# Routing lists with 64-byte records instead of 8-byte ones, filled by one DMA, in an attention-then-mixture-of-experts kernel

## The chip, the cores and the metric

The kernel runs on one core of a Trainium2 chip. The metric is the device time of one launch in microseconds, lower is better. The engines meant below are TensorE (PE in the profile), VectorE (DVE), ScalarE (ACT), GpSimd (POOL) and SyncE (SP). SP issues most of the plain DMAs; GpSimd issues the indirect ones, whose row addresses come from a tile of indices.

## The reference

Linear attention with decay, in float32, for 4 batches, 8 heads, 768 positions and head size 64, followed by a noisy top-2 mixture of experts on the 3072 resulting rows of 512 (8 experts, hidden size 1024):

```python
x = attn_out.transpose(0, 2, 1, 3).reshape(B * S, H * D)      # 3072 x 512
logits = x @ w_gate
noise_scale = np.log1p(np.exp(x @ w_noise))
noisy_logits = logits + noise_scale * noise
top2 = np.argpartition(-noisy_logits, 2, axis=1)[:, :2]
# top2_w: softmax over the two chosen logits
for e in range(E):
    for k in range(2):
        mask = top2[:, k] == e
        h = np.maximum(x[mask] @ w1[e], 0.0)
        out[mask] += top2_w[mask, k, None] * (h @ w2[e])
```

## The kernel before, in words

**Attention** runs in 12 steps of 256 rows (the loop `for t in range(NST)`, a unit u is a step's two chunks of 128 rows). A step transposes k and q of the next unit on TensorE (L298, L311), computes the decayed state (L386, L395, L398) and the scores (L339), multiplies the scores by a decay mask on VectorE (L342), forms the output (L351), transposes it back (L414) and stores the rows to the DRAM tensor `x_tok` (L418). GpSimd scales k for the state (`kdecay`, L327). In each step SP loads k, q and v of the unit three steps ahead.

**Routing** is done in three batches of 8 chunks (`GB`). `gate` (VectorE) computes the noisy logits and the two best experts per row; `weights` (GpSimd, with one reciprocal on VectorE at L507) computes the two softmax weights; `count` and `route` (TensorE and VectorE) give each pair of row and expert a place in that expert's list. Then `scatter_list` (L556) writes the records: one indirect DMA on GpSimd per chunk and choice, so 16 per batch and 48 in all, each with 128 records. A record is the row's number and its weight, `RW` = 2 words of 4 bytes. The lists lie in one DRAM tensor `lst` of 8 lists of 3712 records; before the first scatter they are filled with an out-of-range row number and weight 0 (L876, in step 4, on SP's queue, from the tile `linit`).

**Experts.** Tiles of 128 records are worked on per expert: `load_rec` (L723, L725) loads records from the list, `gather_rows` (L729) fetches the 128 rows of `x_tok` that they name, `trans_rows` (L738, L740, L741) transposes them and splits them into a high and a low part, `gemm1` (L754, L760, L764) and `gemm2` (L792) multiply, and `scatter_out` (L811) adds the result into the output. Expert 0 is worked on in three parts of 2, 2 and 3 tiles (`PARTS0`), each fed by the routing batch of the same number: part 0 is gathered on GpSimd right after the first batch's scatters, at attention step 10 (`GX`); part 1 after the second batch's, part 2 and the other experts after the third. The records reach GpSimd as the indices of a gather only after the list load has landed, and the list load waits for the scatters to land.

**Order.** The schedule is written out by hand: every engine runs its instructions in the order in which the program issues them, and waits come from data only. Several routing instructions are interleaved into the attention steps by `advance(n)`.

**Warm-up.** `keep_warm` (L174) issues matmuls on a tile of zeros, `idle`, 14 of them at the start, so that TensorE is busy while the first loads arrive. `warm` is a one-column tile on which ScalarE does its first activation (L166). A separate tile `zero` of 512 columns, set by GpSimd (L821), is the source of the output's zero fill (L827) and of ScalarE's clearing of gather tiles (L913).

Lines such as L556 are lines of the kernel before; the changed kernel numbers its own up to four lower.

Of the kernel before, what the change touches and what calls it, by code (L numbers as in the profile page):

```python
# [21 lines left out]
FT = mybir.dt.float32  # L22
FR = mybir.dt.float32r
BF = mybir.dt.bfloat16
I32 = mybir.dt.int32
U32 = mybir.dt.uint32
AF = mybir.ActivationFunctionType
OP = mybir.AluOpType
# [7 lines left out]
DM = H * D  # L36
DB = DM // 128
E = 8
# [12 lines left out]
CAP = FULL + TAIL  # L51
STRIDE = 3712
OV = 128
RW = 2
SPS = 6
NST = NCH // 2
NW = NC // 2
# [10 lines left out]
GB = (0, 8, 16, NCH)  # L68
NG = len(GB) - 1
GM = max(GB[i + 1] - GB[i] for i in range(NG))  # L70
# [17 lines left out]
def sub(ap, offset, dims):  # L88
    return bass.AP(tensor=ap.tensor, offset=ap.offset + offset, ap=dims)
# [31 lines left out]
def kernel(  # L121
# [3 lines left out]
    nc = tc.nc  # L125
# [13 lines left out]
    lst = dram.tile([E * STRIDE, RW], I32, name="lst")  # L139
# [21 lines left out]
        nc.sync.dma_start(store[u].rearrange("p h x d -> p h (x d)"),  # L161
                          sub(src, at, [[2 * D, 128], [S * D, H], [1, 2 * D]]))

    warm = ac.tile([128, 1], FT, name="warm")
    nc.vector.memset(warm, 0.0)
    nc.scalar.activation(warm, warm, AF.Copy)  # L166
    idle = ac.tile([128, 384], BF, name="idle")
    nc.vector.memset(idle, 0.0)

    def keep_warm(n):  # L170

# [48 lines left out]
    for nm in ("kt", "qt", "vt"):  # L220
# [7 lines left out]
    ones = consts.tile([128, 128], BF, name="ones")  # L228
    nc.gpsimd.memset(ones, 1.0)
    ST = [ac.tile([128, HP, D], FT, name=f"S{i}") for i in range(5)]  # L230
    iota8 = consts.tile([128, 2, GM, E], FT, name="iota8")
    nc.gpsimd.iota(iota8, pattern=[[0, 2], [0, GM], [1, E]], base=0, channel_multiplier=0,
                   allow_small_or_imprecise_dtypes=True)
    tokf = consts.tile([128, NCH], FT, name="tokf")
    nc.gpsimd.iota(tokf, pattern=[[C, NCH]], base=0, channel_multiplier=1,
                   allow_small_or_imprecise_dtypes=True)
    LI = E * STRIDE // 128 // 4
    linit = ac.tile([128, LI, RW], I32, name="linit")
    nc.gpsimd.memset(linit, BIG)
    nc.gpsimd.memset(linit[:, :, 1:2], 0)  # L240
    sel = consts.tile([128, 2 * E], FT, name="sel")
# [191 lines left out]
    def gate(b):  # L433
        v = nc.vector
        gs = GB[b + 1] - GB[b]
        sh = [128, gs, E]
        t = lambda sh, nm, dt=FT: rp.tile(sh, dt, name=nm)
        pl = PL[b]
        l2 = t([128, gs, 16], "l2")
        v.tensor_copy(l2, pl[:, :gs, :])  # L440
        yield
        zc = t(sh, "zc")
        v.tensor_scalar(zc, l2[:, :, 8:16], 87.0, -87.0, op0=OP.min, op1=OP.max)
        yield
        z = zc.rearrange("p c e -> p (c e)")
        fl = [128, gs * E]
        a = t(fl, "ga")
        v.scalar_tensor_tensor(a, z, -1.0, z, op0=MULT, op1=OP.max)
        yield
        e = t(fl, "ge")  # L450
        yield from exp_neg(v, rp, e, a, fl, "g")
        acc = t(fl, "glacc")
        v.tensor_scalar(acc, e, LOGC[-1], None, op0=MULT)
        yield
        for c in LOGC[-2::-1]:
            v.scalar_tensor_tensor(acc, acc, c, e, op0=ADD, op1=MULT)
            yield
        acc3 = acc.rearrange("p (c e) -> p c e", e=E)
        v.scalar_tensor_tensor(acc3, l2[:, :, 8:16], 0.0, acc3, op0=OP.max, op1=ADD)
        yield  # L460
        nl = t(sh, "nl")
        v.tensor_mul(nl, acc.rearrange("p (c e) -> p c e", e=E), nz[:, GB[b]:GB[b + 1], :])
        yield
        v.tensor_add(nl, nl, l2[:, :, 0:8])
        yield
        mx = t(sh, "mx")
        mi = t(sh, "mi", U32)
        for c in range(gs):
            v.max(mx[:, c, :], nl[:, c, :])
            yield  # L470
        for c in range(gs):
            v.max_index(mi[:, c, :], mx[:, c, :], nl[:, c, :])
            yield
        ei = t([128, 2, gs], "ei")
        v.tensor_copy(ei.rearrange("p r c -> p c r"), mi[:, :, 0:2])
        yield
        oh = t([128, 2, gs, E], "oh")
        v.tensor_tensor(oh, iota8[:, :, :gs, :], ei[:, :, :, None].to_broadcast([128, 2, gs, E]), op=OP.is_equal)
        yield
        ob = t(sh, "ob", BF)  # L480
        v.tensor_add(ob, oh[:, 0], oh[:, 1])
        yield
        RT[b] = dict(mx=mx, ei=ei, oh=oh, ob=ob)

    def weights(b):
        v = nc.gpsimd
        gs = GB[b + 1] - GB[b]
        sh = [128, gs, E]
        r = RT[b]
        t = lambda sh, nm, dt=FT: rp.tile(sh, dt, name=nm)  # L490
        mx = r["mx"]
        rec = r["rec"] = rp.tile([128, gs, 2, RW], I32, name="rec", bufs=2)
        for i in range(2):
            v.tensor_copy(rec[:, :, i, 0], tokf[:, GB[b]:GB[b + 1]])
            yield
        a = t([128, gs], "wa")
        v.tensor_tensor(a, mx[:, :, 0], mx[:, :, 1], op=SUB)
        yield
        v.tensor_scalar(a, a, 87.0, None, op0=OP.min)
        yield  # L500
        e = t([128, gs], "we")
        yield from exp_neg(v, rp, e, a, [128, gs], "w", fused=False)
        s = t([128, gs], "ws")
        v.tensor_scalar(s, e, 1.0, 1e-9, op0=ADD, op1=ADD)
        yield
        yield "sum"
        nc.vector.reciprocal(s, s)  # L507
        yield
        recf = rec.bitcast(FT)
        v.tensor_copy(recf[:, :, 0, 1], s)  # L510
        v.tensor_mul(recf[:, :, 1, 1], e, s)
# [305 lines left out]
            tc.declare_no_dep(st.ins, s.ins, reason="an expert has a token once")  # L817
        out_st.append(st)

    zero = consts.tile([128, DM], FT, name="zero")  # L820
    nc.gpsimd.memset(zero, 0.0)  # L821

    zeros = iter(range(NTOK // 128))

    def zero_out(n):
# [3 lines left out]
    for t in range(NST):  # L829
        u = t + 1  # L830
        if u < NST:
            trans_k(u)
        load(t + 3, "kt")
        if u < NST:
            trans_q(u)
        load(t + 3, "qt")
        if u < NST:
            kv(u)
            state(u)
            advance(FILLS)  # L840
        else:
            store_x(t - 1)
            products(t - 1)
            logits(t - 1)
        intra(t)
        load(t + 3, "vt")
        inter(t, 0)
        evac_o(t)
        if u < NST:
            if t:  # L850
                store_x(t - 1)
                products(t - 1)
            scores(u)
            inter(u, 1)
            if t:
                logits(t - 1)
        if 2 * t in GB[1:]:
            jobs.append(routing(GB.index(2 * t) - 1))
        kdecay(t + 2)
        scatter(SPS)  # L860
        if t in SPLITS:
            split_w(SPLITS[t][0], 0, SPLITS[t][1])
        advance(FILL - (SPLIT if t in SPLITS else 0))
        if t == GX:
            scatter(sum(job[0] == 0 for job in scatters))
            assert "done" in RT[0]
            load_rec(0, 0, nc.gpsimd)
            for j in range(PARTS0[0]):
                gather_rows(0, j, GB[1] * C)
        if t in LOADS:  # L870
            load_w(LOADS[t][0], 0, LOADS[t][1])
        if t == 2:
            nc.sync.dma_start(nz, sub(noise, 0, [[E, 128], [128 * E, NCH], [1, E]]))
        if t == 4:
            for i in range(4):
                nc.sync.dma_start(sub(lst, i * 128 * LI * RW, [[LI * RW, 128], [1, LI * RW]]), linit)  # L876
    products(NST - 1)
    for j in range(2):
        trans_rows(j, TS)
# [232 lines left out]
```

## Time and profile before

| | |
|---|---|
| median of 3 runs | 810.88 us (806.73, 810.88, 1853.96) |
| span of the profiled execution | 803.7 us |
| its own time | not listed apart; the nearest run shown is 806.73 us, 3.0 us above the span |
| PE, DVE, ACT, POOL busy | 743.7, 325.1, 222.4, 290.9 us |
| mean granted TensorE clock | 0.958 |
| DMA moved | 103.49 MB, 92667 packets |
| DMA queue "instruction" (q8) | 49 packets, 0.80 MB |

The span runs from the first to the last instruction. A busy TensorE is not one at its peak, since matmuls are pipelined. Times on the timeline are microseconds from the span's start: attention runs to about 170 us, expert 0 from there to some 275 us with the routing of the second and third batch beside it, the other seven experts to the end. The granted clock is TensorE's share of full speed. "issue" as the releaser of an idle time means that the profile shows nothing that the engine waited for.

### The profile page before, as it was taken

The numbers are of one execution on the slowest core, as the hardware profiler recorded it, in microseconds if no ns is written. First come the engines' busy times: TensorE is split into PE (matmuls) and PEld (weight loads), VectorE is DVE, ScalarE is ACT, GpSimd is POOL, SyncE is SP. The second block draws the span as 40 slices with busy tenths as digits, with TensorE's granted clock in tenths as the row PEclk, the third lists the DMA queues.
The fourth block names the chain that finished last, engine by engine and source line by source line (L and its number), as shares of the span: only waits on it lengthen the run. The fifth ranks groups of instructions, "written<-read, shape, count | busy, mean of one in ns | idle before, by whom it ended". The sixth has DMA issues, their size and how long they took to land. (4 is left out here: it accounts for less than half of the span.)

```text
span 803.7 us, 15438 instructions
## 1 busy us (share of the span) xinstructions
PE 743.7 (93%) x6122; PEld 626.0 (78%) x6122; DVE 325.1 (40%) x742; ACT 222.4 (28%) x381; POOL 290.9 (36%) x474
## 2 busy tenths in 40 slices
PE   6999898685959999999999999999999999999993
PEld 4888776474758889889888888888788888889882
DVE  5555654353412554436243424433342443335210
ACT  0445443241111343214222321322142232214100
POOL 1321155547755145442344234333413433221221
PEclk8899998697979999999999999999999999999997
DMA  8899974130908165344243424343442544240110
GB/s 170 189 266 253 238 194 125 27 107 5 337 16 255 66 172 152 118 144 140 68 144 112 152 81 155 120 118 104 144 132 78 150 133 132 64 128 26 59 53 21
DMA packets 92667, 103.49 MB, mean 129 GB/s; under 512 B 39203, under 2 KB 65315, under 8 KB 92592
## 3 DMA queue, kind: packets, MB, share of 16 engines
q1 hardware_dynamic: 79456, 66.25, 30.7%
q0 software_dynamic: 13136, 36.23, 13.9%
q8 instruction: 49, 0.80, 0.4%
q14 instruction: 26, 0.21, 0.1%
HBM read 77.78 MB, written 25.93 MB: 129 GB/s over the span
## 5 line engine op out<-in xcount | busy, mean ns | idle before, releaser
L754 PE MATMUL pS<-xth,w1h 128*128 128x512 f32 (+3 forms) x544 | 182.8, 336 | 6.2 <-issue 4.6
L754 PE MATMUL pS<-xtl,w1h 128*128 128x512 f32 (+3 forms) x544 | 181.7, 334 | 7.1 <-issue 5.2
L754 PE MATMUL pS<-xth,w1l 128*128 128x512 f32 (+3 forms) x544 | 181.8, 334 | 3.7 <-issue 3.7
L764 DVE SCALAR_TENSOR_TENSOR ht<-pS,ht 128x256 fp32r<-128x256 f32 (+3 forms) x176 | 76.4, 455 | 167.9 <-ACT ht L760 150.2
L811 POOL DMA_INDIRECT out_dram<-ot,rec x46 | 65.2, 1418 | 185.9 <-DVE ot L804 174.8
L792 PE MATMUL pO<-w2h,ht 128*128 128x512 f32 x384 | 127.8, 403 | 2.6 <-issue 2.3
L792 PE MATMUL pKV<-w2h,ht 128*128 128x512 f32 x384 | 125.6, 398 | 0.0
L760 ACT ACTIVATE ht<-pS 128x512 fp32r<-128x512 f32 (+3 forms) x136 | 65.4, 484 | 207.8 <-PE pS L754 154.7
L754 PEld LDWEIGHTS pS<-xth,w1l 128*128 128x128 f32 x544 | 103.6, 190 | 16.7 <-issue 7.9
L754 PEld LDWEIGHTS pS<-xtl,w1h 128*128 128x128 f32 x544 | 103.6, 190 | 15.4 <-issue 4.4
L754 PEld LDWEIGHTS pS<-xth,w1h 128*128 128x128 f32 x544 | 103.6, 190 | 14.6 <-issue 3.6
L792 PEld LDWEIGHTS pO<-w2h,ht 128*128 128x128 f32 x384 | 73.2, 191 | 20.0 <-issue 3.8
L740 ACT ACTIVATE xth<-pS 128x512 fp32r<-128x512 f32 (+2 forms) x53 | 29.8, 572 | 204.0 <-PE pS L738 203.8
L792 PEld LDWEIGHTS pKV<-w2h,ht 128*128 128x128 f32 x384 | 72.3, 188 | 16.3
L792 PE MATMUL pO<-w2l,ht 128*128 128x512 f32 x192 | 76.7, 399 | 1.4 <-issue 1.3
L792 PE MATMUL pKV<-w2l,ht 128*128 128x512 f32 x192 | 75.7, 394 | 0.0
L776 POOL DMA_INDIRECT pv<-out_dram,rec x46 | 47.1, 1023 | 31.0 <-issue 31.0
L327 POOL TENSOR_TENSOR kd<-kt,Mk 128x512 f32<-128x512 f32 x24 | 24.8, 1056 | 91.2 <-PE pR L386 49.5
L729 POOL DMA_INDIRECT xg<-x_tok,rec x46 | 50.1, 1088 | 19.2 <-issue 14.6
L342 DVE TENSOR_TENSOR at<-pS,Mk 128x512 f32<-128x512 f32 x48 | 30.4, 685 | 52.7 <-PE pS L339 32.5
L556 POOL DMA_INDIRECT lst<-rec,dest x48 | 46.8, 975 | 10.8 <-issue 9.9
L804 DVE SCALAR_TENSOR_TENSOR ot<-pO,rec,pv 128x512 f32<-128x512 f32 x21 | 15.8, 751 | 82.7 <-PE pO L792 82.7
(189 smaller groups left out, 963.8 us busy)
## 6 DMA issues: line engine op xcount, KB each, us to landing
wst<-in_moe_w_dram SPq DMA_DIRECT2D x48, 512.0 KB
wst<-in_moe_w_dram SPq DMA_DIRECT2D x32, 256.0 KB
kt<-in_k_dram SPq DMA_DIRECT2D x12, 512.0 KB
qt<-in_q_dram SPq DMA_DIRECT2D x24, 256.0 KB
vt<-in_v_dram SPq DMA_DIRECT2D x12, 512.0 KB
x_tok<-xc SPq DMA_DIRECT2D x24, 256.0 KB
out_dram<-zero SPq DMA_DIRECT2D x24, 256.0 KB
lst<-rec,dest POOLq DMA_INDIRECT x48
```

Source lines behind the costliest of these rows:

```text
L327: nc.gpsimd.tensor_mul(kd[:, :, s], kt[:, :, s], mask(s, slice(0, HP), slice(C - 1, C)).to_broadcast([128, HP, 2, D]))
L342: nc.vector.tensor_mul(at[:, s], ps[s], mask(s, slice(2 * r, 2 * r + 2), slice(0, C)))
L556: st = nc.gpsimd.indirect_dma_start(out=lst, out_offset=bass.IndirectOffsetOnAxis(ap=r["dest"][:, i, c:c + 1], axis=0), in_=r["rec"][:, c, ...
L729: nc.gpsimd.indirect_dma_start(out=XG[t][:size(e, t)], out_offset=None, in_=x_tok[:rows, :], in_offset=bass.IndirectOffsetOnAxis(ap=REC[e, ...
L740: nc.scalar.activation(hi, p, AF.Copy)
L754: nc.tensor.matmul(p, W1[a][d][:, fs], xt(b, cs)[:, d], start=(d == 0 and i == 0), stop=(d == DB - 1 and i == 2))
L760: nc.scalar.activation(ht(e, 0, f, cs), p, AF.Relu)
L764: nc.vector.scalar_tensor_tensor(ht(e, 1, f, c), p[:, r], 0.0, ht(e, 0, f, c).bitcast(FT), op0=OP.max, op1=SUB)
L776: nc.gpsimd.indirect_dma_start(out=PV[t][:size(e, t), :], out_offset=None, in_=out, in_offset=bass.IndirectOffsetOnAxis(ap=REC[e, t][:, 0: ...
L792: nc.tensor.matmul(p, ht(e, a, f, cs), W2[b][f // 2][:, f % 2, :], start=(i == 0), stop=(i == len(terms) - 1))
L804: nc.vector.scalar_tensor_tensor(o, p, w, pv, op0=MULT, op1=ADD)
L811: st = nc.gpsimd.indirect_dma_start(out=out, out_offset=bass.IndirectOffsetOnAxis(ap=REC[e, t][:, 0:1], axis=0), in_=o, in_offset=None, bo ...
```

## The change

A record takes 16 words, 64 bytes, of which the first two mean what they meant. The row number is copied to all 16 words, then the weight is written over the second; scatters and list loads move whole records. The fill of the lists, which is now 1.9 MB, is one DMA that reads a tile of 8 records 29 times per partition, in pieces of 512 bytes, in the place of four DMAs of 58 KB. To hold the larger record tiles, others shrink or are shared: the iota of expert numbers is one row that is read with a step of zero, two tiles of the gate reuse the names of dead ones, and `idle`, `warm` and `zero` become one tile, set by VectorE at the start.

```diff
-RW = 2
+RW = 16
...
-    warm = ac.tile([128, 1], FT, name="warm")
-    nc.vector.memset(warm, 0.0)
-    nc.scalar.activation(warm, warm, AF.Copy)
-    idle = ac.tile([128, 384], BF, name="idle")
-    nc.vector.memset(idle, 0.0)
+    zero = consts.tile([128, DM], FT, name="zero")
+    nc.vector.memset(zero, 0.0)
+    nc.scalar.activation(zero[:, :1], zero[:, :1], AF.Copy)
+    idle = zero.bitcast(BF)[:, :384]
...
-    iota8 = consts.tile([128, 2, GM, E], FT, name="iota8")
-    nc.gpsimd.iota(iota8, pattern=[[0, 2], [0, GM], [1, E]], base=0, channel_multiplier=0,
+    iota8 = consts.tile([128, 1, 1, E], FT, name="iota8")
+    nc.gpsimd.iota(iota8, pattern=[[0, 1], [0, 1], [1, E]], base=0, channel_multiplier=0,
...
-    LI = E * STRIDE // 128 // 4
-    linit = ac.tile([128, LI, RW], I32, name="linit")
+    LI = E * STRIDE // 128
+    LB = 8
+    linit = ac.tile([128, LB, RW], I32, name="linit")
...
-        acc = t(fl, "glacc")
+        acc = t(fl, "gn")
...
-        nl = t(sh, "nl")
+        nl = t(fl, "gu").rearrange("p (c e) -> p c e", e=E)
...
-        v.tensor_tensor(oh, iota8[:, :, :gs, :], ei[:, :, :, None].to_broadcast([128, 2, gs, E]), op=OP.is_equal)
+        v.tensor_tensor(oh, iota8.to_broadcast([128, 2, gs, E]), ei[:, :, :, None].to_broadcast([128, 2, gs, E]), op=OP.is_equal)
...
-            v.tensor_copy(rec[:, :, i, 0], tokf[:, GB[b]:GB[b + 1]])
+            v.tensor_copy(rec[:, :, i, :], tokf[:, GB[b]:GB[b + 1], None].to_broadcast([128, gs, RW]))
...
-    zero = consts.tile([128, DM], FT, name="zero")
-    nc.gpsimd.memset(zero, 0.0)
...
-            for i in range(4):
-                nc.sync.dma_start(sub(lst, i * 128 * LI * RW, [[LI * RW, 128], [1, LI * RW]]), linit)
+            nc.sync.dma_start(sub(lst, 0, [[LI * RW, 128], [LB * RW, LI // LB], [1, LB * RW]]),
+                              linit.rearrange("p l w -> p (l w)")[:, None, :].to_broadcast([128, LI // LB, LB * RW]))
```

SP's queue at attention step 4, before: the fill of the lists (`lst<-linit`) stands between a weight load (`wst`) and the k, q and v loads of step 8's unit.

```order
L418 DMA x_tok<-xc 128x512 x2
L679 DMA wst<-in_moe_w_dram 128x1024
L876 DMA lst<-linit 128x116 x4
L161 DMA kt<-in_k_dram 128x8x128
L157 DMA qt<-in_q_dram 128x8x64 x2
L161 DMA vt<-in_v_dram 128x8x128
```

The same place now:

```order
L418 DMA x_tok<-xc 128x512 x2
L679 DMA wst<-in_moe_w_dram 128x1024
L872 DMA lst<-linit 3712x1x128
L161 DMA kt<-in_k_dram 128x8x128
L157 DMA qt<-in_q_dram 128x8x64 x2
L161 DMA vt<-in_v_dram 128x8x128
```

One DMA of 3712 pieces of 128 words stands where four of 128 pieces of 116 words stood; what follows keeps its order.

GpSimd's queue in attention step 0 and after, before (`kd` is the scaled k, `xg` a gather tile, `rec` a batch's records, `tokf` the row numbers):

```order
L614 MEMSET xg_359 128x512
L614 MEMSET xg_360 128x512
L623 MEMSET rank 1x8
L626 MEMSET tail 1x16
L821 MEMSET zero 128x512
L327 TENSOR_TENSOR kd<-kt,Mk 128x4x128 x16
L494 CAST rec<-tokf 128x8 x2
```

And now:

```order
L614 MEMSET xg_357 128x512
L614 MEMSET xg_358 128x512
L623 MEMSET rank 1x8
L626 MEMSET tail 1x16
L327 TENSOR_TENSOR kd<-kt,Mk 128x4x128 x16
L494 CAST rec<-tokf 128x8x16 x2
```

The setting of `zero` is gone from here (it is VectorE's first instruction now), and each copy of the row numbers writes 16 words per record.

## The prediction

> **What bounds the kernel now.** I read the page's slices first, then the busy time by stretches, then each engine's timeline in the stretches where TensorE has gaps. The stretches (columns: us, busy us and count on PE, PEld, DVE, ACT, POOL; then granted clock, DMA share, GB/s):
>
> ```profile
> 20.00:100.00 80.00, 75.24 (x1743) 65.89 (x1740) 46.42 (x126) 38.76 (x72) 17.78 (x21) 0.96 0.97 238
> 100.00:128.00 28.00, 26.02 (x641) 23.34 (x641) 17.28 (x65) 13.18 (x25) 11.68 (x31) 0.94 0.73 190
> 132.00:152.00 20.00, 9.11 (x47) 4.50 (x45) 1.58 (x3) 0.00 (x0) 14.90 (x28) 0.58 0.17 32
> 187.00:201.00 14.00, 6.07 (x13) 3.33 (x14) 1.55 (x7) 1.42 (x4) 9.17 (x17) 0.60 0.05 9
> 201.00:220.00 19.00, 17.52 (x106) 14.65 (x105) 9.84 (x52) 3.31 (x8) 14.20 (x41) 0.94 1.02 352
> 223.00:236.00 13.00, 4.88 (x19) 3.67 (x19) 1.16 (x4) 1.32 (x4) 7.67 (x15) 0.66 0.02 1
> 236.00:260.00 24.00, 22.90 (x128) 20.21 (x127) 5.43 (x13) 3.01 (x7) 14.37 (x19) 0.97 0.78 218
> 260.00:780.00 520.00, 520.00 (x2666) 439.91 (x2665) 203.81 (x339) 140.97 (x225) 171.35 (x232) 1.00 0.37 114
> ```
>
> TensorE sets the end from 260 us on: it is busy all 520 us, so whatever comes earlier in front of that stage moves the end one for one. Before it there are three holes, 132 to 152, 187 to 201 and 223 to 236, in which TensorE did 47, 13 and 19 matmuls while the DMA engines stood nearly still. Its own timeline, from three places (idle time before an instruction and its releaser in brackets):
>
> ```profile
> 120.23 1.98 PE L339 MATMUL pS<-qT,kT 64*64 64x128 f32 x64
> 130.21 2.05 PE L339 MATMUL pS<-qT,kT 64*64 64x128 f32 x47
> 160.27 1.98 PE L339 MATMUL pS<-qT,kT 64*64 64x128 f32 x64
> ...
> 183.79 0.28 PE L754 MATMUL pS<-xtl,w1h 128*128 128x256 f32 x1
> 183.91 0.28 PE L754 MATMUL pS<-xth,w1l 128*128 128x256 f32 x1
> ...
> 231.30 0.37 PE L754 MATMUL pS<-xtl,w1h 128*128 128x256 f32 x1 [1.03 <-issue]
> 233.40 0.37 PE L754 MATMUL pS<-xth,w1l 128*128 128x256 f32 x1 [1.73 <-issue]
> ...
> 235.18 0.42 PE L754 MATMUL pS<-xth,w1l 128*128 128x256 f32 x1
> 235.39 0.42 PE L754 MATMUL pS<-xth,w1h 128*128 128x256 f32 x1
> ...
> 237.52 0.28 PE L754 MATMUL pS<-xtl,w1h 128*128 128x256 f32 x1
> ```
>
> The score matmuls of L339 come once per attention step: 9.98 us between the first two, 30.06 to the third, so the first hole costs 20.1 us. Inside a hole one matmul follows another after 2.10 us (231.30 to 233.40) where 0.12 is normal (183.79 to 183.91), and the releaser is "issue": no engine and no semaphore holds it. What all three holes share is on GpSimd's timeline:
>
> ```profile
> 104.17 0.35 POOL L494 CAST rec<-tokf 128x8 int32<-128x8 f32 x2
> ...
> 130.49 0.97 POOL L556 DMA_INDIRECT lst<-rec,dest  x1 [0.21 <-issue]
> ...
> 148.21 0.96 POOL L556 DMA_INDIRECT lst<-rec,dest  x1 [0.22 <-issue]
> 151.04 0.59 POOL L725 DMA_DIRECT2D recz<-lst  x1 [1.87 <-DMA lst<-rec,dest]
> 153.37 1.80 POOL L729 DMA_INDIRECT xg<-x_tok,recz  x1 [1.74 <-DMA recz<-lst]
> 155.46 1.00 POOL L729 DMA_INDIRECT xg<-x_tok,recz  x1 [0.30 <-issue]
> ...
> 165.53 0.20 POOL L497 TENSOR_TENSOR wa<-mx 128x8 f32<-128x8 f32 x1 [8.71 <-DVE mx L469]
> ...
> 177.00 0.20 POOL L510 COPY rec<-ws 128x8 f32<-128x8 f32 x1 [4.09 <-DVE ws L507]
> ...
> 231.25 0.96 POOL L556 DMA_INDIRECT lst<-rec,dest  x1 [0.22 <-issue]
> ...
> 240.55 0.97 POOL L729 DMA_INDIRECT xg<-x_tok,recz  x1 [0.30 <-issue]
> 241.83 1.02 POOL L729 DMA_INDIRECT xg<-x_tok,rec  x1 [0.31 <-issue]
> ```
>
> Each hole lies in a burst of 16 scatters into the lists (L556: 128 records of 8 bytes each, one every 1.27 us) and ends 2 to 3 us after it. It is not the pace of indirect DMAs that hurts: the gathers of 2 KB rows come as fast (240.55, 241.83), and in 236 to 260 TensorE is busy 22.90 of 24 us. What is peculiar to the bursts is 8-byte writes to neighbouring addresses in memory: each list grows by about 16 adjacent records per scatter (128 tokens over 8 experts). My reading is that these partial writes back up in memory, and that TensorE's supply of instructions, which the page lists as a DMA queue of its own, is caught behind them. The trace shows the coincidence; the cause it does not show.
>
> **The change, part by part.** I sum against the profiled execution: span 803.7 us. The nearest of the runs shown, 806.73, lies 3.0 above it, and I use 806.7 as its own time; the median, 810.88, lies 4.2 higher.
>
> Records of 64 bytes. A scatter still has 128 destinations, so I keep GpSimd's pace of 1.27 us. Each record now fills a 64-byte slot alone, so no two records of a scatter share one. The forecast is that the holes go. That is not worth their sum, because behind TensorE stands a second chain: scatter, list landed, list loaded, gather, transposes, and GpSimd walks it at its own pace. Followed step by step, with what TensorE and the list loads do in before:
>
> ```profile
> 170.01 1.09 PE L738 MATMUL pS<-identf,xg 128*128 128x128 f32 x8
> ...
> 249.62 1.43 PE L738 MATMUL pS<-identf,xg 128*128 128x128 f32 x12
> ...
> 235.41 0.86 SPq L725 DMA_DIRECT2D recz<-lst  x2
> ...
> 211.05 0.20 DVE L507 RECIPROCAL ws<-ws 128x8 f32<-128x8 f32 x1 [2.72 <-POOL ws L504]
> ```
>
> 1. Without the first hole TensorE stands before the first gathered tiles at 170.01 - 20.1 = 149.9. The second tile's gather is issued at 155.46 whatever TensorE does. Its flight I estimate at 3.1 us: 2.33 from issue to use of a list (151.04 to 153.37) plus 0.74 for 256 KB at the 352 GB/s of the row 201 to 220. So the transposes end near 155.5 + 0.1 (longer list load, below) + 3.1 + 0.5 = 159.2 instead of 171.1: 11.9 us earlier, and TensorE has waited some 7 us.
> 2. After such a wait it starts cold. At 235.18 matmuls follow each other at 0.21 us, and full pace is back at 237.52: 2.3 us at 0.21 for 0.12 loses 1.0. That leaves 10.9 for the second burst. GpSimd itself could start it earlier: 177.00 - 8.71 - 4.09 = 164.2, both waits being for DVE work that TensorE had held up.
> 3. Second burst, load, two gathers, weights, third burst: GpSimd's pace, less 0.5 for added work (below): 10.4.
> 4. The third burst's last scatter ends at 232.2, and the load that waits for it starts at 235.41, 3.2 us later. The first burst's wait was 1.87. I take that: 11.7, less 0.1 for the load: 11.6.
> 5. The last gather of this expert, 240.55, is then issued at 228.95, lands at 232.0, and the remaining transposes end near 232.4 instead of 251.05: 18.6 us. TensorE is there first: the reciprocal at 211.05 moves to about 200.7; from there to 249.62 it needs 38.6 us less the third hole, which is 13.0 us less 19 matmuls of 0.12, or 10.7: 228.6, and 229.6 with a cold start.
> 6. A cold start again, 1.0: 17.6.
>
> [...] The row at 237.52 shows 2.3 us, which I use.
>
> If the holes only halve, steps 1 to 5 lose little: TensorE waits 7 us at step 1 anyway. If they go and landings get faster still, up to 3 us come on top.
>
> The fill. Four DMAs of 58 KB become one of 1.9 MB, in pieces of 512 bytes, at the same place of SP's queue:
>
> ```profile
> 75.39 3.18 SPq L876 DMA_DIRECT2D lst<-linit  x4
> 78.68 0.39 SPq L161 DMA_DIRECT2D kt<-in_k_dram  x1
> ...
> 98.56 1.51 PE L298 MATMUL pS<-identf,kt 128*128 128x128 f32 x12
> ```
>
> 1.66 MB more at 238 GB/s (row 20 to 100, DMA share 0.97) is 7.0 us of all DMA engines. Behind it in the queue stand the k, q and v loads of step 8, then x stores and weights. The k load issued at 78.68 is used at 98.56, 19.9 us later, and from 100 us the DMA share is 0.73, which leaves 7.6 us spare. I take 1.5, between 0 (hidden) and 7.0 (all of it felt).
>
> Small parts. The list loads carry 32 KB for 4: 28 KB at 238 GB/s, 0.1 each. The token copies (L494) write 128 elements a partition for 8. Two took 0.35 us; a 512-element GpSimd operation takes 1.06, by this row of the page's groups:
>
> ```profile
> L327 POOL TENSOR_TENSOR kd<-kt,Mk 128x512 f32<-128x512 f32 x24 | 24.8, 1056 | 91.2 <-PE pR L386 49.5
> ```
>
> So the pair costs between 0.35 and 2.1; I take 0.4 more. One tile for idle operand and zeros: TensorE's warm-up now waits for ScalarE's first activation, not for DVE's memset.
>
> ```profile
> 1.14 4.52 PE L174 MATMUL pR<-idle 128*128 128x384 bf16 x14 [1.14 <-DVE idle L168]
> ...
> 2.01 0.20 ACT L166 ACTIVATE warm<-warm 128x1 f32<-128x1 f32 x1
> ...
> 16.13 0.44 PE L386 MATMUL pS<-vt,kd 64*64 64x64 f32 x2 [3.82 <-DMA vt<-in_v_dram]
> ```
>
> It starts at 2.21 instead of 1.14: 1.1 us, hidden by the 3.82 us in which TensorE later waits for v; without that cover, 1.1. The smaller iota, the dropped GpSimd memset and the reuse of gate tiles by DVE, which both wrote and reads them in order, I cost at nothing: none of them stands before a wait of TensorE.
>
> Sum: 806.7 - 17.6 + 1.5 = 790.6; I say 790.
>
> **The rivals.** First, the holes stay. For it: the trace has no 64-byte writes, and the cause is inferred. The time is then 806.7 + 1.5 + 0.5, about 809. [...]
>
> Second, slower: the fill holds up SP's queue. The four small fills took 3.18 us to issue for 237 KB; by bytes the large one takes 25 us. It decides once k's load at 78.68 slips past its use at 98.56, that is above 20 us. With 25.4 - 3.2 = 22.2 us of delay and 3 us of flight the load comes some 6 us late, and so do q and v behind it: 6 to 10 us on the path. With the holes kept that is 815 to 819, with the holes gone 796 to 800. Against it: the 512 KB load behind it was issued in 0.39 us, so issue time does not go by bytes.
>
> Third, the holes shrink by less than half, or a part of them belongs to indirect DMA as such: 797 to 803.
>
> **How the numbers follow.** Chances: holes gone 0.57, its own range 783 to 798; holes stay 0.23; fill on the path 0.12, half of it with the holes kept; holes shrunk a little 0.08. The range reaches from 783 to 812: left out are the slower half of the second rival, the tail of the first and a gain above 24 us, together under 0.2. What this kernel's measurement tells from no change is about 2%, 16 us: below about 793, 2% under the middle of the runs at 806.73 and 810.88, the change is faster. Of the first case some four fifths lie there, and a little of the others: 0.48. Slower by over 2%, above 825, needs the fill at its worst with the holes kept: 0.09. The rest, 0.43, is within 2%.
>
> **What would show it.** If right: no stretch in which L754 or L339 matmuls come 0.7 to 2 us apart with releaser "issue" during L556; instead TensorE waits for gathered tiles or ACT's copies of them (L738 near 157 and 229); the gap from the last L556 to its list load under 2 us; the 260 to 780 stage unchanged, 17 us earlier. If wrong: holes of the same length beside bursts of 16 scatters; or, for the fill, TensorE or GpSimd waiting for k, q or v between 80 and 110 us, and scatters longer than 1.27 us.

## The result and the profile after

The changed kernel takes 812.4 us (median of 8 runs, 812.18 to 814.97) against 807.35 before: a ratio of 1.0064, 95% interval 1.0044 to 1.0083. Two later comparisons give 1.0040 (1.0012 to 1.0067) and 1.0027 (1.0007 to 1.0047). So it is slower, by 0.3 to 0.6%, some 2 to 5 us; the forecast was 790, its range 783 to 812. The profiled execution has a span of 810.6 us, 6.9 more than before. Its stretches, with windows moved to where the holes now lie (columns as above):

```profile
20.00:100.00 80.00, 75.79 (x1758) 66.56 (x1760) 46.28 (x131) 40.09 (x74) 17.50 (x20) 0.97 1.03 250
100.00:128.00 28.00, 23.34 (x547) 20.57 (x544) 14.23 (x48) 11.44 (x23) 10.65 (x29) 0.94 0.79 216
133.00:154.00 21.00, 8.27 (x59) 4.30 (x50) 1.42 (x3) 0.64 (x1) 15.56 (x30) 0.60 0.17 52
189.00:204.00 15.00, 5.66 (x15) 3.32 (x15) 2.34 (x10) 1.23 (x4) 9.90 (x19) 0.60 0.08 24
204.00:223.00 19.00, 17.81 (x96) 14.43 (x96) 9.51 (x51) 3.11 (x8) 14.36 (x41) 0.87 0.95 348
227.00:239.00 12.00, 4.86 (x15) 3.00 (x14) 0.80 (x3) 0.81 (x4) 6.87 (x13) 0.60 0.04 7
239.00:260.00 21.00, 19.90 (x101) 17.12 (x101) 5.11 (x11) 2.65 (x7) 10.18 (x12) 0.90 0.72 201
260.00:780.00 520.00, 520.00 (x2674) 439.86 (x2673) 203.69 (x341) 141.66 (x227) 173.99 (x238) 1.00 0.37 116
```

All three holes are still there: 59, 15 and 15 matmuls in 21, 15 and 12 us. From 260 us on nothing has changed. TensorE's timeline shows both where the holes stand and a pause ahead of them:

```profile
112.53 0.39 PE L351 MATMUL pO<-at,vt 64*64 64x128 f32 x4
116.82 0.48 PE L351 MATMUL pKV<-at,vt 64*64 64x128 f32 x2 [3.90 <-issue]
...
122.14 1.98 PE L339 MATMUL pS<-qT,kT 64*64 64x128 f32 x64
132.12 2.08 PE L339 MATMUL pS<-qT,kT 64*64 64x128 f32 x47
...
150.31 0.37 PE L351 MATMUL pKV<-qTs,S 64*64 64x128 f32 x1 [1.66 <-issue]
151.03 0.46 PE L351 MATMUL pO<-qTs,S 64*64 64x128 f32 x1 [0.35 <-issue]
...
163.25 1.98 PE L339 MATMUL pS<-qT,kT 64*64 64x128 f32 x64
...
172.98 1.09 PE L738 MATMUL pS<-identf,xg 128*128 128x128 f32 x8
...
255.15 1.43 PE L738 MATMUL pS<-identf,xg 128*128 128x128 f32 x12
```

The step with the first hole takes 31.13 us from one group of score matmuls to the next (132.12 to 163.25; before 30.06). The transposes of the first gathered tiles (172.98) are 3.0 us later than before, those of the third part (255.15) 5.5 us, the end 6.9 us. GpSimd's timeline:

```profile
102.86 0.53 POOL L494 CAST rec<-tokf 128x128 int32<-128x128 f32 x2
...
130.88 1.23 POOL L556 DMA_INDIRECT lst<-rec,dest  x1 [0.19 <-POOL spacer L555]
...
150.08 0.96 POOL L556 DMA_INDIRECT lst<-rec,dest  x1 [0.22 <-issue]
152.81 0.59 POOL L725 DMA_DIRECT2D recz<-lst  x1 [1.77 <-DMA lst<-rec,dest]
...
234.23 0.96 POOL L556 DMA_INDIRECT lst<-rec,dest  x1 [0.22 <-issue]
```

Sixteen scatters still take 19.2 us from first start to last (130.88 to 150.08), the pace of before; the wider copies of the row number took 0.53 us for a pair. SP's queue, where the fill stands:

```profile
75.14 0.63 SPq L872 DMA_DIRECT2D lst<-linit  x1
76.85 6.57 SPq L161 DMA_DIRECT2D kt<-in_k_dram  x1
83.52 2.42 SPq L157 DMA_DIRECT2D qt<-in_q_dram  x2
...
236.34 0.86 SPq L725 DMA_DIRECT2D recz<-lst  x2
```

The fill itself is issued in 0.63 us, but the k load behind it takes 6.57 us where it took 0.39, and is through at 83.42 instead of 79.07.

### The profile page after: what moved, and what is told of

It reads as the page before. It is cut to its first block, busy times and chain, and to the rows that moved or that the text cites. A ratio compares the mean times of both kernels' runs of the same rounds, so it can differ in the third digit from the quotient of the medians.

```text
span 810.6 us, 15432 instructions
## 1 busy us (share of the span) xinstructions
PE 746.7 (92%) x6122; PEld 628.1 (77%) x6122; DVE 324.7 (40%) x741; ACT 222.1 (27%) x381; POOL 289.5 (36%) x473
## 5 line engine op out<-in xcount | busy, mean ns | idle before, releaser
L754 PE MATMUL pS<-xtl,w1h 128*128 128x512 f32 (+3 forms) x544 | 182.9, 336 | 8.0 <-issue 6.1
L754 PE MATMUL pS<-xth,w1h 128*128 128x512 f32 (+3 forms) x544 | 183.7, 338 | 6.6 <-issue 4.9
L754 PE MATMUL pS<-xth,w1l 128*128 128x512 f32 (+3 forms) x544 | 182.0, 335 | 4.5 <-issue 4.4
L754 PEld LDWEIGHTS pS<-xtl,w1h 128*128 128x128 f32 x544 | 104.2, 192 | 18.4 <-issue 7.4
L754 PEld LDWEIGHTS pS<-xth,w1h 128*128 128x128 f32 x544 | 104.2, 192 | 17.5 <-issue 6.7
L754 PEld LDWEIGHTS pS<-xth,w1l 128*128 128x128 f32 x544 | 104.2, 192 | 13.7 <-issue 4.9
L556 POOL DMA_INDIRECT lst<-rec,dest x48 | 46.6, 972 | 10.8 <-issue 9.8
```

The lines of the kernel that those rows point to most:

```text
L556: st = nc.gpsimd.indirect_dma_start(out=lst, out_offset=bass.IndirectOffsetOnAxis(ap=r["dest"][:, i, c:c + 1], axis=0), in_=r["rec"][:, c, ...
L754: nc.tensor.matmul(p, W1[a][d][:, fs], xt(b, cs)[:, d], start=(d == 0 and i == 0), stop=(d == DB - 1 and i == 2))
```

## The experiments

Two theories stood at the start. **T1**, that of the prediction: scattered writes that are too small back up in memory, and 64 bytes are still too small. **T2**: a long run of indirect DMAs on GpSimd starves TensorE of instructions, whatever it moves. T2 came from a count in the traces: from the first scatter of a burst to the first pair of matmuls 0.6 us or more apart, TensorE starts 78 and 69 matmuls in the first two bursts of before and 70 and 68 after, though the two bursts meet matmuls of quite different length. It looks as if supply breaks off when the burst begins, and TensorE then uses up what is buffered. (In the third burst a gap of 1.01 us, between the transposes of L738 and the matmuls of L754 that use them, comes after 11 matmuls in before and 17 after, and spoils the count.)

### Eight variants of the scatter

Each replaces the two operands of L556, on top of the changed kernel:

```diff
 # e1_gather: reads instead of writes
-            out=lst, out_offset=bass.IndirectOffsetOnAxis(ap=r["dest"][:, i, c:c + 1], axis=0),
-            in_=r["rec"][:, c, i, :], in_offset=None)
+            out=r["rec"][:, c, i, :], out_offset=None, in_=lst,
+            in_offset=bass.IndirectOffsetOnAxis(ap=r["dest"][:, i, c:c + 1], axis=0))
 # e2_none: no scatter at all
 # e3_direct: a plain DMA on GpSimd's queue
+        st = nc.gpsimd.dma_start(sub(lst, (i * STRIDE + (GB[b] + c) * 128) * RW, [[RW, 128], [1, RW]]), r["rec"][:, c, i, :])
 # e4_wide: 2048 bytes per row into another tensor `wide`
+            out=wide, out_offset=bass.IndirectOffsetOnAxis(ap=r["dest"][:, i, c:c + 1], axis=0),
+            in_=zero, in_offset=None)
 # e5_apart, e6_dense, e7_512, e8_256: the same with in_=zero[:, :n],
 # rows of 64 bytes 2048 apart (indices times 32); of 64 bytes, dense; of 512, dense; of 256, dense
```

> The 48 list scatters become 48 indirect gathers: the same instruction on GpSimd with the same 128 addresses, but it reads 64 bytes from each list row into the record tile and writes nothing to memory. The lists keep their first fill, so the experts compute on empty rows and the total is not to be compared; what counts is TensorE from the first burst on. Theory T1 (small writes to memory back up, so that transfers behind them are late): no write is left, the three holes go; TensorE is busy over 95% of 130 to 240 us outside its real waits, and no stretch of matmuls 0.7 to 2.1 us apart is seen inside a burst. Theory T2 (a long back-to-back run of indirect DMAs on GpSimd starves TensorE of instructions, whatever they move): all three holes stay, each beginning after 55 to 80 matmuls counted from the burst's first gather, matmuls again 0.7 to 2.1 us apart, TensorE busy 8 to 10 us in the 20 us of the first burst.

> The 48 list scatters are left out (the records are made but not written; the lists keep their first fill, the experts compute on empty rows, and the total is not to be compared). Both theories expect the three holes to go; the run prices them: by the trace after, TensorE is busy 8.75 of 20 us, 5.89 of 14 us and 7.14 of 13 us in them, so about 11 + 8 + 6 = 25 us less idle time of TensorE between 128 and 240 us, less what other waits take over. If matmuls stay 0.7 to 2.1 us apart at the same places of the program without any scatter, both theories are wrong and the cause is TensorE's own code.

> The 48 list scatters become 48 plain DMAs from GpSimd's queue: 128 rows of 64 bytes each to fixed list rows in order, no addresses read (the records land in wrong rows, so the experts compute on other rows and the total is not to be compared). T1 (small writes back up): 64-byte writes as before, the holes stay at their places and sizes. T2 in its narrow form (the indirect instruction's own work on GpSimd starves TensorE): the holes go, TensorE is busy over 95% in the bursts. T2 in its wide form (any long run of DMAs issued from GpSimd): the holes stay, but as long as the burst now lasts, some 16 x 0.7 us = 11 us where a direct DMA takes about 0.6 us to issue (the one direct DMA of this queue, the list load, took 0.59 us).

> The 48 scatters write 2048 bytes per row (zeros) to another memory tensor instead of 64 bytes to the lists; same addresses, same number of instructions and rows, 32 times the bytes (12.6 MB in all). The lists keep their first fill, so the total is not to be compared. T1 (writes under 512 bytes are slow at the memory): no write is small any more, the holes go, or at least matmuls in a burst come under 0.7 us apart from memory's side; T2: the holes stay as they are, onset after 55 to 80 matmuls, matmuls 0.7 to 2.1 us apart, TensorE busy 8 to 10 us of the first burst's 20; if the DMA engines become the limit (16 x 262 KB in 20 us is 210 GB/s), the burst may stretch, but not the spacing in it.

> The 48 scatters write 64 bytes (zeros) per row into another memory tensor, each row 2048 bytes from the next, so that no two rows lie in the same 512 bytes. The lists keep their first fill, so the total is not to be compared; what counts is TensorE in the three bursts. Three readings of the runs so far (reads, 2 KB rows and 64-byte rows in order make no hole): A, the size: every scattered write under 512 bytes costs, so the holes stay (TensorE idle 18 us of the 20 to 25 us of the first burst, matmuls 0.7 to 2.1 us apart). B, the sharing: several small writes from different DMA engines into the same 512 bytes cost, so the holes go. C, the place: the lists' own place in memory costs, so the holes go.

> As the run with rows 2048 bytes apart, but the 64-byte rows lie one behind the other, as in the lists, in another memory tensor (lists keep their fill, the total is not to be compared). A (size) and B (sharing): the holes are as after the change, about 18, 10 and 9 us of idle TensorE. C (place in memory): the holes go.

> The 48 scatters write 512 bytes of zeros per row, rows one behind the other in another memory tensor (lists keep their fill, the total is not to be compared). By A and B with a granule of 512 bytes every row is a whole granule and the holes go. If they stay, the granule is larger than 512 bytes, or the 2048-byte rows were saved by something else, such as their time on the DMA engines spreading the writes out.

> The 48 scatters write 256 bytes of zeros per row, rows one behind the other in another memory tensor (lists keep their fill, the total is not to be compared). A with a granule of 512 bytes: each write is still less than a granule, the holes stay as they are, since the number of writes sets them. B with 512 bytes: two writes share a granule instead of eight, the holes stay but shrink to well under half. If they go altogether, the granule is 256 bytes or less.

They ran as two sets of four; a set is a group of runs taken together, with the kernel before among them. There is no hole in any of them: from 128 to 155 us TensorE is busy 20.12 to 26.44 of 27 us in the eight, 14.27 in the changed kernel. The stretch of the first burst, for reads (e1_gather; columns as in the stretches above):

```profile
128.00:155.00 27.00, 22.79 (x576) 19.38 (x576) 18.62 (x66) 14.30 (x26) 20.04 (x35) 0.99 0.37 107
```

for no scatter at all (e2_none):

```profile
128.00:155.00 27.00, 24.86 (x594) 21.11 (x591) 18.60 (x59) 16.11 (x30) 11.54 (x40) 1.00 0.33 105
```

and for 64-byte rows, dense, in another tensor (e6_dense):

```profile
128.00:155.00 27.00, 26.44 (x648) 23.41 (x644) 20.48 (x64) 14.01 (x26) 17.54 (x31) 1.00 0.45 144
```

At first sight the gather speaks for T1 and against T2. But e6_dense does to memory what the changed kernel does, and has no hole either, which speaks against T1 as well. And the kernel before took 796.68 and 797.43 us in these two sets, 10 us less than in the result above. So the next question was the kernel itself.

### The kernels again, the record size alone, and another order

> The changed kernel itself once more, on the chip of this comparison. In the runs with other destinations or other forms of the scatter no hole was seen, not even with 64-byte rows laid as in the lists but in another memory tensor. If the holes belong to the program (the scatters into the lists themselves), this run shows three stretches of matmuls 0.7 to 2.1 us apart after 55 to 80 matmuls of each burst, as on record, and the ratio to before is 1.004 to 1.009. If they belong to a chip or to one execution, they may be gone, and the span then falls by 20 to 25 us.

> The kernel before once more, on the same chip, for its profile. Holes of the program: three, as on record. Holes of a chip or an execution: gone here when they are gone in the changed kernel's profile on this chip.

The record size alone is put back:

```diff
-RW = 16
+RW = 2
...
-    LB = 8
+    LB = 58
```

> The changed kernel with records of 8 bytes as before the change and the fill of 0.24 MB in one DMA in pieces of 464 bytes as before; all other edits stay. If the loss of 0.6% is the larger fill (its 1.9 MB at the DMAs' full load, then TensorE's longer pause at 112 to 117 us) and the wider casts, the time is that of before within 0.3% (ratio 0.997 to 1.003). If the merged tiles and the single fill DMA carry the loss, it stays at 1.004 to 1.009.

The scatters of a step are put ahead of its decay product:

```diff
-        kdecay(t + 2)
         scatter(SPS)
+        kdecay(t + 2)
```

> The changed kernel with the step's scatters put ahead of its decay product on GpSimd, so that the first six scatters of the first burst run in GpSimd's idle 115 to 128 us, and the burst that is left has ten. If each scatter into the lists takes TensorE's instructions away for a time, whenever it comes, the idle time moves but does not fall by more than a few us (ratio to the changed kernel 0.995 to 1.0). If a hole needs a long run of scatters, after TensorE's buffer of 60 to 75 matmuls is used up, the first hole shrinks by the six scatters that it lost, 6 x 1.27 = 7.6 us (ratio to the changed kernel about 0.99).

In this set before takes 809.38 us (27 runs), after 813.70, ratio 1.0040 (1.0012 to 1.0067). Both profiles have the three holes: the kernels' own, and repeatable here.

With 8-byte records the time is 808.73, ratio to before 0.9985 (0.9970 to 1.0001). So the whole loss goes with the record size, that is with the larger fill, the wider copies and list loads; the merged tiles, the single fill DMA and the smaller iota cost nothing that can be seen. Four places of the profiles (us), to see where it enters:

| | before | before again | 8-byte records | after | after again | after, third |
|---|---|---|---|---|---|---|
| first scatter (L556) | 128.96 | 126.54 | 128.76 | 130.88 | 131.54 | 133.58 |
| first gathered tiles transposed (L738) | 170.01 | 167.88 | 170.17 | 172.98 | 173.26 | 175.25 |
| third part transposed (L738) | 249.62 | 250.62 | 251.43 | 255.15 | 255.18 | 257.18 |
| span | 803.7 | 804.7 | 805.5 | 810.6 | 810.8 | 812.9 |

On average the changed kernel is 4.3 us late at the first scatter, 5.7 at the third part, 7.2 at the end (one profiled execution each, with 1 to 3 us between executions of one kernel; by medians the loss is 3 to 5). Over half of it is there before a single scatter has run. Upstream of that point stand the fill and one pair of copies of 0.53 us, so the fill is a suspect. It is not shown to be the payer: no run changed it alone, and the profiles do not agree on where the time goes. In the first pair the changed kernel is not late at 112.5 us, and 1.7 us late behind a pause of TensorE that follows. Before (after, shown above: 112.53 and 116.82):

```profile
112.75 0.39 PE L351 MATMUL pO<-at,vt 64*64 64x128 f32 x4
115.12 0.48 PE L351 MATMUL pKV<-at,vt 64*64 64x128 f32 x2 [1.98 <-issue]
```

The two later profiles of the changed kernel have this pause at its length before, 2.25 and 2.52 us from start to start (2.25 and 2.53 in the two of before), but come to it later, at 115.31 and 118.62 us (before: 112.87 and 111.58; 8-byte records: 114.62). The later of them was behind already before the fill was issued: its 1000th matmul starts at 62.5 us, that of the other five between 57.4 and 59.1.

The other order takes 814.54, no better than 813.70. GpSimd in it:

```profile
119.84 1.23 POOL L556 DMA_INDIRECT lst<-rec,dest  x1 [0.51 <-POOL spacer L555]
...
126.42 0.95 POOL L556 DMA_INDIRECT lst<-rec,dest  x1 [0.23 <-issue]
136.16 2.05 POOL L327 TENSOR_TENSOR kd<-kt,Mk 128x512 f32<-128x512 f32 x2 [8.79 <-PE pR L386]
138.41 1.05 POOL L556 DMA_INDIRECT lst<-rec,dest  x1 [0.16 <-issue]
...
149.86 0.95 POOL L556 DMA_INDIRECT lst<-rec,dest  x1 [0.21 <-issue]
```

Six scatters do run in what was idle time. But TensorE reaches its first gap after 77 matmuls, just when the six are done, its decayed state comes later, and with it the decay product (136.16 for 128.60; 4.1 us of this is the pause above, which ended at 120.89 in this execution). Under the ten that are left TensorE runs dry after 55 matmuls, and they end where the sixteen did, at 149.86 against 150.08. The expectation that a shorter run shortens the hole fell; that idle time only moves held.

### Source and destination, one at a time

Between e6_dense (no hole) and the changed kernel (holes) two things differ in the program: the tile that is read and the tensor that is written.

```diff
 # x1_rec_wide: the records, into another tensor
-            out=lst, out_offset=bass.IndirectOffsetOnAxis(ap=r["dest"][:, i, c:c + 1], axis=0),
+            out=wide, out_offset=bass.IndirectOffsetOnAxis(ap=r["dest"][:, i, c:c + 1], axis=0),
 # x2_far_lst: a constant tile, into the lists
-            in_=r["rec"][:, c, i, :], in_offset=None)
+            in_=far, in_offset=None)
```

> The 48 scatters write the records themselves, 64 bytes per row, rows one behind the other, but into another memory tensor of the lists' size and form; the lists keep their first fill, so the experts compute on empty rows and the total is not to be compared. Against the run that wrote zeros there (no hole) only the source differs, against the changed kernel (three holes) only the tensor written. If reading the record tile is what hurts, the holes are there (TensorE busy about 15 of 27 us between 128 and 155 us); if it is the lists themselves (their place in memory, or that they were filled and are read later), they are gone (26 of 27 us).

> The 48 scatters write into the lists themselves, at the same rows, but from one constant tile that holds the number of an empty row, so the lists read as empty, the experts compute on empty rows and the total is not to be compared. Against the changed kernel only the source differs. Holes as on record (about 15 of 27 us busy between 128 and 155 us): it is the destination. No holes: it is the source, the record tile.

The holes are there with both, first x1_rec_wide, then x2_far_lst:

```profile
128.00:155.00 27.00, 14.63 (x223) 9.80 (x215) 5.74 (x19) 4.19 (x8) 20.70 (x36) 0.69 0.15 46
```

```profile
128.00:155.00 27.00, 15.00 (x213) 10.00 (x203) 6.58 (x21) 4.00 (x8) 19.62 (x35) 0.67 0.15 46
```

So neither operand decides. What was left is that before took 809.62 us in this set and 797 in the sets without holes.

### The variants in a set with holes

Two of the first variants again, unchanged:

> Once more the kernel with 48 indirect gathers in place of the scatters (reads of 64 bytes, nothing written; lists keep their fill, the total is not to be compared). All runs without holes came from two sets of runs in which the kernel before took 796.7 and 797.4 us; all with holes from sets in which it took 807 to 810 us. If the set decides, holes go with the time of before: at 807 to 810 us T1 (scattered small writes) expects no hole here and T2 (any run of indirect DMAs on GpSimd) expects three, with TensorE busy about 15 of 27 us between 128 and 155 us; at 796 to 798 us neither is told.

> Once more the kernel whose scatters write 64-byte rows of zeros into another memory tensor (lists keep their fill, the total is not to be compared). It had no hole, and the same kernel with the records as source had three in another set of runs. If the source tile decides, no hole here either; if the set of runs decides, three holes when before takes 807 to 810 us here, and none at 796 to 798 us.

Before takes 809.62 us here, and both variants have the holes. They also take 830.05 and 831.19 us, where the same two programs took 780.58 and 786.24 in the sets without holes: 49 and 45 us more (single runs), against some 12 for before; what makes up so much was not followed. Reads (e1b_gather), then 64-byte rows elsewhere (e6b_dense):

```profile
128.00:155.00 27.00, 15.12 (x244) 10.12 (x241) 7.45 (x28) 6.09 (x11) 19.36 (x35) 0.71 0.22 59
```

```profile
128.00:155.00 27.00, 15.18 (x247) 10.33 (x245) 7.22 (x27) 5.83 (x11) 19.63 (x35) 0.71 0.17 54
```

TensorE in the first burst of e1b_gather:

```profile
147.49 0.37 PE L351 MATMUL pO<-qTs,S 64*64 64x128 f32 x1 [1.04 <-issue]
148.21 0.37 PE L351 MATMUL pKV<-qTs,S 64*64 64x128 f32 x1 [0.35 <-issue]
150.31 0.37 PE L351 MATMUL pKV<-qTs,S 64*64 64x128 f32 x1 [1.73 <-issue]
```

The same spacing, 0.72 and 2.10 us, with nothing written to DRAM (the rows go into the record tile on the chip). That settles T1: writes to DRAM are not needed for a hole. The gaps begin after 67 and 62 matmuls (e1b_gather) and 71 and 60 (e6b_dense), in T2's range.

The last two runs were the kernel once more and the plain DMAs:

> The changed kernel once more, for the set of runs that it falls into. By the runs so far the holes go with the set: in a set in which before takes 807 to 810 us they are there for scatters and gathers alike; in a set at 796 to 798 us this run should show no stretch of matmuls 0.7 us or more apart inside a burst before 340 matmuls, and TensorE busy over 22 of 27 us between 128 and 155 us. If before takes 797 us and the three holes are here all the same, the set is not the reason.

> Once more the kernel with 48 plain DMAs from GpSimd's queue in place of the scatters (records land in wrong rows, the total is not to be compared). In a set in which before takes 807 to 810 us: if the indirect form's work on GpSimd starves TensorE, no stretch of matmuls 0.7 us or more apart is seen in the three runs of plain DMAs, which come 0.66 us apart; if any run of DMAs from GpSimd does, the stretches begin after 55 to 80 matmuls as with scatters and gathers and last to the end of each run, some 11 us from its start. In a set at 796 to 798 us it tells nothing.

Before takes 809.69 us here. The changed kernel has its holes again (a_third), at 813.08 us, ratio 1.0027 (1.0007 to 1.0047):

```profile
128.00:155.00 27.00, 16.25 (x255) 11.39 (x253) 7.93 (x29) 6.20 (x11) 19.00 (x34) 0.73 0.20 63
```

With plain DMAs (e3b_direct) there is none:

```profile
128.00:155.00 27.00, 24.83 (x589) 20.93 (x588) 17.71 (x58) 15.06 (x28) 17.88 (x54) 1.00 0.39 126
```

```profile
132.92 0.59 POOL L557 DMA_DIRECT2D lst<-rec  x1
133.51 0.55 POOL L557 DMA_DIRECT2D lst<-rec  x1
```

These are, in the same set and on the same queue, 128 writes of 64 bytes per DMA, twice as fast one after the other (0.66 us apart on average, 132.07 to 141.92, for 1.28 with the scatters of the changed kernel), and TensorE is busy 24.83 of 27 us; the first gap of 0.6 us or more, which is a step's ordinary wait for ScalarE, comes after 347 matmuls. Of these, 236 start while the sixteen DMAs run, so this run is long enough to count; in the second and third run of plain DMAs only 72 and 50 start, which tells little. The program with plain DMAs takes 767.21 us here and took 764.97 in the first set: without indirect scatters the sets differ little. From 128 to 260 us TensorE is busy 124 us here and 97 in the changed kernel of the same set: the holes and what follows from them are worth up to 27 us of TensorE's time, an upper bound, because with the records in other rows the later waits differ too.

Together (345 and 347 end at the same ordinary wait of a step for ScalarE, not at a hole):

| run | L556 is | before in its set, us | TensorE busy, 128 to 155 us | matmuls to the first gap, bursts 1 and 2 |
|---|---|---|---|---|
| e1_gather | gather | 796.68 | 22.79 | 345; a data wait |
| e4_wide | scatter, 2 KB | 796.68 | 25.94 | 345; a data wait |
| e6_dense | scatter, 64 B, elsewhere | 797.43 | 26.44 | 345; a data wait |
| after again | scatter, 64 B | 809.38 | 15.01 | 70; 68 |
| u1_rw2 | scatter, 8 B | 809.38 | 15.38 | 73; 68 |
| x1_rec_wide | scatter, 64 B, elsewhere | 809.62 | 14.63 | 71; 63 |
| e1b_gather | gather | 809.62 | 15.12 | 67; 62 |
| e6b_dense | scatter, 64 B, elsewhere | 809.62 | 15.18 | 71; 60 |
| e3b_direct | plain DMA, 64 B | 809.69 | 24.83 | 347; a data wait |

What is shown: where holes exist, indirect DMAs in a run of sixteen go with them, whichever way the data go; plain ones from the same queue do not, in the one execution of them in a set with holes. All rows there were of 8 or 64 bytes; larger ones were not run in such a set. What stays open is why two sets of runs had none. The program and even the chip listed (the same for the first set and for the sets of x1_rec_wide and e1b_gather) do not tell them apart, and the pace of GpSimd hardly does: an indirect DMA takes 0.978 us on average in e1_gather and 0.961 in e1b_gather, 0.985 in e6_dense and 0.980 in e6b_dense. e1_gather has one of 1.55 us for 0.95 in the first burst (at 136.78), and whether as cause or as consequence no run tells. The time of before does tell them apart, and its profile was not taken there. So the rows of e4_wide, e5_apart, e7_512 and e8_256 say nothing on the size of a write, and their readings in size, sharing and place are void; the 512 bytes that their expectations take as a limit were the author's assumption, which no run shows.

The traces also show where the supply is not cut. Instructions come in packets of 16 KB on queue q8, 49 in an execution. That they are TensorE's is read from their pace: in the changed kernel, from 170 us on, 92 to 139 matmuls start between one packet and the next. From 128 to 155 us it has two (packets, MB, share of the 16 DMA engines):

```profile
q8 instruction: 2, 0.03, 0.4%
```

The second starts at 134.66 us and takes 0.88 us, so it has landed when the first gap begins at 136.03. Up to 154 us TensorE starts 32 matmuls, a part of what one packet holds, and the next packet is not due. In the second and third hole 9 and 28 matmuls start between a packet and the end of the hole. A late packet looks different: at the pause of 112 to 117 us, 188 matmuls had started since the packet before, the new one landed at 115.4, and TensorE went on at 116.82. So in a hole, as far as the trace shows, the instructions have been brought in and do not reach TensorE; what holds them there stays open.

## Why the prediction was wrong

**The bound** was read rightly: TensorE is busy 520 of 520 us from 260 on in both kernels, and what came late ahead of it (5.5 us at the third part's transposes) came out at the end (6.9).

**The step that failed** is "The forecast is that the holes go", and under it the reading that partial writes back up in memory. The records now fill 64 bytes each, and the three holes have their old spacing and length. Reads make the same holes, and 64-byte writes by plain DMAs make none, so writes to DRAM are neither needed nor enough. Nor is the instruction queue caught behind anything that the trace shows: its packet has landed, at 135.54 us, when the first hole begins at 136.03. What the runs show in the place of the writes is the run of sixteen indirect DMAs itself. What led there was the sentence that the pace of indirect DMAs does not hurt, because gathers come as fast and TensorE stays busy beside them. They come in runs of 7, some 9 us, in which TensorE starts 40 matmuls; by the count above supply has to fail for 55 to 78 before it shows. By that count the counter-example was too short to be one.

**The chain of six steps** and its 17.6 us had no occasion: it follows from holes that are gone. The nearest figure to it is the kernel before in the two sets without holes, 10 to 13 us faster than in the others (one run in each), if it had none there itself. Only step 4's assumption met a measurement, that the list load's wait of 3.2 us after the last scatter falls to 1.87 with the holes. It fell to 1.15 (234.23 + 0.96 to 236.34) with the holes in place, so that wait does not belong to them.

**The fill**, 1.5 us in the sum between ends of 0 and 7.0, and the 0.5 us for copies and list loads are too little together: the record size as a whole costs 5.0 us (813.70 less 808.73). Which of them was mis-sized no run tells. The second rival's mechanism did occur in small: k's load was through 4.4 us later, behind the fill, and it was this load, not the fill, whose issue took long (6.57 us), which the argument against that rival had not allowed for. Its limit of 20 us was not reached. The pause of TensorE at 112 to 117 us (3.90 us, "issue") is no mark of the fill: before has it too, with 1.98 us.

**The small parts** held: the pair of copies went from 0.35 to 0.53 us, less than the 0.4 added; TensorE's warm-up starts at 2.26 instead of 1.14 us and the wait for v behind it hides that (its first dependent matmul at 16.33 for 16.13).

**The rivals.** The first, holes stay, came true, at 0.23; its 809 is 3 us short. It had the right outcome for the records, but the size of a write does not carry the holes: they are there with 8 bytes (u1_rw2, TensorE busy 15.38 of 27 us) and with 64 (after again, 15.01), and the plain DMAs write 64-byte rows too and make no hole (24.83). The third rival had named indirect DMA as such, and dismissed it to 0.08 as a part of the holes; in the sets with holes the runs point to it for all of them.

## What to carry to other kernels

An engine that stops with nothing to wait for may be starved by what another engine does; count its instructions from the start of the suspected run to the first gap, since a nearly constant count under different lengths of instruction (here 55 to 78 matmuls) points to a buffer that is no longer refilled, an inference that no trace here shows directly. A counter-example in the same trace (here the gathers, with 40 matmuls) only counts if it lasts as long as that count. When variants are compared one by one, put the unchanged kernel's own profile into every set, or the set is taken for the variant.

## What was not expected of the hardware

Inside a hole most matmuls start on a grid of about 0.71 us (gaps of 0.69 to 0.72, 1.39 to 1.43 and 2.08 to 2.13 us in before and after, 0.72 and 2.10 in e1b_gather), while GpSimd issues a DMA every 1.27 us. The buffer that TensorE seems to live on is an estimate from the count above: 55 to 78 matmuls, each with its weight load (6122 of each on the page of after).

In two sets of runs no program had holes, among them two that had them when they were run again, with GpSimd at nearly the same pace (0.978 us per indirect DMA in e1_gather without holes, 0.961 in e1b_gather with them); the kernel before was 10 to 13 us faster there. Plain DMAs of 128 rows from GpSimd took 0.54 to 0.59 us each after the first (e3b_direct), indirect ones 0.95 (e1_gather). A load of 512 KB queued behind one DMA of 3712 pieces took 6.57 us to issue (after), and 0.39 behind four DMAs of 58 KB (before).
